# Second-weight combinations by column halves in five regions, and gating remainders one group later

## The chip, the cores and the metric

The kernel runs on one core of one Trainium2 chip. The metric is the device time of one execution in microseconds (us). Engines are named as the profile names them: PE (TensorE), DVE (VectorE), ACT (ScalarE), POOL (GpSimd) and SP (SyncE, whose queue issues every DMA here). Each engine takes its instructions strictly in the order of its own queue.

## The reference

Four batches of 576 positions go through attention, a gated block and a feed-forward block.

```python
x = attention(q, k, v)                     # 8 heads of 64: 4 local (32 back), 4 strided (32 apart)
h = gelu(x @ w_in)                         # 512 -> 1024
u, v = h[..., :512], h[..., 512:]
v = layer_norm(v) * g_ln
x = x + (u * (w_sg @ v + b_sg)) @ w_out    # w_sg: 576 x 576 over positions
y = layer_norm(x) * g_2
out = x + relu(y @ w_ch1) @ w_ch2          # 512 -> 2048 -> 512
```

## The kernel before

**Precision.** Nearly every product is made of three matmuls in a reduced format: an operand is split into a rounded part and a remainder. ACT copies the value into the rounded part, then DVE subtracts it from the value for the remainder (`split`, line 185).

**Attention and gating.** While the gated block of one batch runs, the attention of the next is laid between its groups. For each pair of heads `attn_s` makes scores on PE (`ps_sc`, L373), adds masks on DVE (L383, L384), which carries the scores from PSUM to SBUF, and takes the maxima (`mx`). `attn_e` exponentiates on ACT (L408) and normalises on DVE (`pt`, L418). `attn2` transposes on PE (`ps_t`, L447). The scores have two PSUM banks (`ps_s`), so a pair's scores can start only when the masks of the pair before have been added. `sg_group` makes eight groups per batch: PE fills `ps_g`, DVE multiplies (`z`, L598), ACT copies (`gt`, L599), DVE subtracts (`gt`, L600).

**Feed-forward.** The tokens come in three chunks of 768. In every chunk the first product is made by a seven-product scheme over 2x2 blocks (`product`, L886, seven of six matmuls a pair of column blocks, `pair`, eight pairs). Between a pair's products ACT copies partial sums out of PSUM: `s1` (L938), `u2` (L947) and `u4` (L953). The next product into that bank, `a`, waits for the copy. DVE forms `late` (L954) from the other bank, `b`, to which the pair's last product (number 4) is then added. Chunks 0 and 1 use plain second products (`ch2`); each ends in a late loop of sixteen steps, one `h` (L891, L892) and 12 matmuls a step. Chunk 2 uses seven-product combinations of the second weights too. These are made during chunk 1 by `combine2`, eight times: DVE adds the two parts of `w2` to the whole weight in `stg` (L715), forms combinations in place (L719 to L722), ACT rounds all of it into another part of `stg` (L187), DVE writes the remainder over the sums (L188), and SP stores both in DRAM (`w2_scratch`, L726). One place in `stg` serves all eight.

**Order.** The code is written in program order. A list scheduler then fixes one static order for each engine by its own estimate of when things are ready, so an edit in one place moves instructions in others.

Of the kernel before, what the change touches and what calls it, by code (L numbers as in the profile page):

```python
# [12 lines left out]
F32 = mybir.dt.float32  # L13
F32R = mybir.dt.float32r
U32 = mybir.dt.uint32
AF = mybir.ActivationFunctionType
# [25 lines left out]
NSC = 3  # L42
NLATE = 10
WX = {1: (0, 2, 0), 2: (4, 2, 1), 7: (1, 2, 5), 4: (5, 2, 2), 5: (8, 1, 3), 6: (10, 1, 4), 3: (12, 1, 6)}
WX2 = {1: (0, 2, 0), 2: (4, 2, 2), 7: (1, 2, 1), 4: (5, 2, 2), 5: (8, 1, 0), 6: (10, 1, 1), 3: (12, 1, 3)}
COMBINE_F = {12: 7}
ORDER2 = (1, 7, 2, 6, 5, 4, 3)
XTAGS = (0, 4, 1, 5, 2, 3, 6)
NT = B * S
# [106 lines left out]
def mixer_kernel(ctx: ExitStack, tc: tile.TileContext, io, out):  # L156
# [172 lines left out]
            out=vt[:vrows, :vcols],  # L329
            in_=io["v_l" if local else "v_s"][b, p % (NP // 2)].rearrange("p i h d -> p (i h d)"))  # L330

    pend = {}

    def attn_s(b, p):
        local = p < NP // 2
        n = NLB if local else NSG
        w = LW if local else GW
        if (b, p) not in kv:
            attn_load(b, p)
        qk = kv.pop((b, p))  # L340
        if local:
            p3 = at.tile([P, NLB * LW], F32, tag="pt", name="pt").rearrange("p (n w) -> p n w", w=w)
        else:
            p3 = pts[p % 2].rearrange("p (n w) -> p n w", w=SLOT)[:, :, :w]
        mx = small.tile([P, NSG], F32, tag="mx", name="mx")
        sm = small.tile([P, NSG], F32, tag="sm", name="sm")
        on_pe = b < MASK_PE
        todo = []
        for o in range(2):
            m = (n + 1 - o) // 2  # L350
            if b == 0 and p in START_D:
                ps = ps_d.tile([P, 512], F32, tag="d", name="ps_sc")
            else:
                ps = ps_s.tile([P, 512], F32, tag="s", name="ps_sc")
            lo = 1 if local and o == 0 else 0
            todo.append((slice(o, n, 2), m, ps[:, :m * w].rearrange("p (n w) -> p n w", w=w), lo))
        mk = mask_l[:, 1, :] if local else mask_s
        mkr = mask_lr[:, 1, :] if local else mask_sr
        if on_pe:
            for sl, m, ps3, lo in todo:  # L360
                if lo:
                    nc.tensor.matmul(ps3[:, 0, :], lhsT=ident_r, rhs=mask_lr[:, 0, :], start=True, stop=False,
                                     skip_group_check=True)
                nc.tensor.matmul(ps3[:, lo:, :], lhsT=ident_r,
                                 rhs=mkr.unsqueeze(1).to_broadcast([P, m - lo, w]), start=not lo, stop=False,
                                 skip_group_check=True)
        for i in range(n):
            for h in range(2):
                hs_ = slice(64 * h, 64 * h + 64)
                k0 = KO + QB * i if local else KS + GW * i  # L370
                q0 = QB * i if local else GW * i
                r0 = 64 * (h ^ (i % 2))
                nc.tensor.matmul(todo[i % 2][2][r0:r0 + 64, i // 2, :], lhsT=qk[hs_, q0:q0 + QB],  # L373
                                 rhs=qk[hs_, k0:k0 + w], start=not on_pe, stop=True,
                                 skip_group_check=True)
        chunks = []
        for sl, m, ps3, lo in todo:
            if on_pe:
                masked = ps3
            else:  # L380
                masked = p3[:, sl, :]
                if lo:
                    nc.vector.tensor_tensor(out=p3[:, 0, :], in0=ps3[:, 0, :], in1=mask_l[:, 0, :], op=ALU.add)  # L383
                nc.vector.tensor_tensor(  # L384
                    out=masked[:, lo:, :], in0=ps3[:, lo:, :],
                    in1=mk.unsqueeze(1).to_broadcast([P, m - lo, w]), op=ALU.add)
            nc.vector.tensor_reduce(out=mx[:, sl], in_=masked, op=ALU.max, axis=AX.X)
            if p in SHIFTED[min(b, 1)]:
                nc.vector.tensor_tensor(out=p3[:, sl, :], in0=masked,
                                        in1=mx[:, sl].unsqueeze(2).to_broadcast([P, m, w]), op=ALU.subtract)  # L390
            else:
                nc.vector.tensor_scalar_mul(mx[:, sl], mx[:, sl], -SCALE)
            chunks.append((sl, m, masked))
        pend[b, p] = (p3, n, w, mx, sm, chunks)
# [188 lines left out]
    def sg_group(b, i):  # L583
        u = us[b]
        d, hf = i // 2, i % 2
        if i == 0:
            gts[b] = dw.tile([P, 2, KD, S], F32R, tag="gt", name="gt")
        gt = gts[b]
        dsl = slice(d * P, (d + 1) * P)
        cs = slice(hf * SH, (hf + 1) * SH)  # L590
        ps = ps_d.tile([P, 512], F32, tag="d", name="ps_g")
        o = ps[:, :SH]
        for s in range(4):
            mm3(o, vn[:, 0, s, dsl], vn[:, 1, s, dsl], wsg[:, 0, s, cs], wsg[:, 1, s, cs], s == 0, False)
        nc.tensor.matmul(o, lhsT=vn[:, 1, 4, dsl], rhs=wsg4l[:, cs], start=False, stop=False)
        nc.tensor.matmul(o, lhsT=vn[:, 0, 4, dsl], rhs=wsg4h[:, cs], start=False, stop=True)
        z = dn.tile([P, SH], F32, tag="z", name="z")
        nc.vector.tensor_tensor(out=z, in0=o, in1=u[:, d, cs], op=ALU.mult)  # L598
        nc.scalar.activation(gt[:, 0, d, cs], z, AF.Copy)  # L599
        nc.vector.tensor_tensor(out=gt[:, 1, d, cs], in0=z, in1=gt[:, 0, d, cs], op=ALU.subtract)  # L600

    y_t = {}

    def y_group(b, i):
        gt, x32 = gts[b], x32s[b]
# [101 lines left out]
        (split_later if i + 1 < NW else split)(  # L707
            w[:, 0].rearrange("p k f -> p (k f)"), w[:, 1].rearrange("p k f -> p (k f)"), f)

    def combine2(i):  # L710
        stg = big["stg"]
        c = stg[:, 0:1792].bitcast(F32)
        wf = c[:, 0:1024].rearrange("p (k e r f) -> p k e r f", k=2, e=2, r=2)
        w = w2[i].rearrange("p a k f -> p a (k f)").bitcast(F32)
        nc.vector.tensor_tensor(out=c[:, 0:1024], in0=w[:, 0], in1=w[:, 1], op=ALU.add)  # L715
        s = c[:, 1024:1792].rearrange("p (s e f) -> p s e f", s=3, e=2)
        a11, a21, a12, a22 = wf[:, 0, :, 0], wf[:, 0, :, 1], wf[:, 1, :, 0], wf[:, 1, :, 1]
        tt = nc.vector.tensor_tensor
        tt(out=s[:, 0], in0=a21, in1=a22, op=ALU.add)  # L719
        tt(out=s[:, 1], in0=s[:, 0], in1=a11, op=ALU.subtract)  # L720
        tt(out=a21, in0=a11, in1=a21, op=ALU.subtract)
        tt(out=s[:, 2], in0=a12, in1=s[:, 1], op=ALU.subtract)  # L722
        hi, lo = stg[:, 1792:3584].bitcast(F32R), stg[:, 0:1792].bitcast(F32R)
        split(hi, lo, c)
        for h, src in enumerate((hi, lo)):
            nc.sync.dma_start(out=w2_d[:, :, i, h, :].rearrange("n p f -> p n f"),  # L726
                              in_=src.bitcast(F32).rearrange("p (n f) -> p n f", f=P))

    w2s, slices = {}, {}
# [156 lines left out]
                nc.tensor.matmul(o, lhsT=w[:, a, n0 + nk * k, :], rhs=x[:, c, k, :], start=first and k == 0 and n == 0,  # L886
                                 stop=k == 1 and n == 2, skip_group_check=True)

    def to_h(src):
        h = big["h"].tile([P, 2, TH], F32R, tag="h", name="h")  # L890
        nc.scalar.activation(h[:, 0, :], src, AF.Relu)  # L891
        nc.vector.scalar_tensor_tensor(out=h[:, 1, :], in0=src, scalar=0.0, in1=h[:, 0, :],  # L892
                                       op0=ALU.max, op1=ALU.subtract)
        return h
# [37 lines left out]
    def pair(sc, i, role, mid):  # L932
# [11 lines left out]
        tt(out=c11, in0=c, in1=s1, op=ALU.add)  # L944
        product(sc, i, a, 6, False)
        u2 = tmp("u2")
        nc.scalar.activation(u2, a, AF.Copy)  # L947
        h1 = to_h(c11)
        if i:
            ch2(sc, 0, f1 - 2, 1 - role)  # L950
        product(sc, i, a, 5, False)
# [16 lines left out]
    def steps_at(sc, i, role):  # L968
        if sc + 1 < NSC:
            for step in NORM_AT[sc > 0].get(i, ()):  # L970
                norm(sc + 1, step, role)

    def last_stage():
        for sc in range(NSC - 1):
            role = sc % 2
            for i in range(NW):
                pair(sc, i, role, lambda: steps_at(sc, i - 0.5, role))
                if sc == 0:
                    if i + 2 < NW:
                        prepare(len(units[done[0]:]) if i + 3 == NW else 6)  # L980
                        if i < NW - 2:
                            keep(i + 2)
                else:
                    if i + 2 < NW:
                        fetch(i + 2)
                    if i < NW - len(COMBINE_F):
                        combine2(i)
                steps_at(sc, i, role)
                if i == NW - 3:
                    residual(sc, 0)  # L990
                if i >= NW - 2:
                    rsqrt(sc, i + 2 - NW)
# [6 lines left out]
            for f in range(NF):  # L999
                hs[f] = to_h(late(f))  # L1000
                if f in EXPAND_AT:
                    expand(sc + 1, EXPAND_AT.index(f))
                if f == 4:
                    residual(sc, 1)
                if sc and f in COMBINE_F:
                    combine2(COMBINE_F[f])
                ch2(sc, 1, f, role)
            for d in range(KD):
                leave(sc, 1, d)
# [288 lines left out]
```

## Time and profile before

| quantity | value |
|---|---|
| median of 3 runs | 681.0 us (679.6, 681.0, 681.93) |
| profiled execution, own time | 683.11 us |
| its span | 681.3 us |
| PE busy, share of the span | 655.6 us, 96% |
| DVE busy | 510.1 us, 75% |
| ACT busy | 377.9 us, 55% |

Busy time is the union of an engine's instructions. A gap of PE is time that can be won. [...]

### The profile page before, as it was taken

Reading aid. Unit: us, or ns where it says so; the run is one execution under the profiler, and the core shown is the slowest. Engines: PE = TensorE matmul, PEld = TensorE weight load, DVE = VectorE, ACT = ScalarE, POOL = GpSimd, SP = SyncE. Lnnn points to the kernel's source line nnn. Section 1 sums busy time; section 2 is a strip of 40 time slices with the busy share of each in tenths; the row PEclk is TensorE's granted clock in tenths of the full one; section 3 lists DMA queues with packets and bytes.
Section 4 is the critical chain, followed back from the end, with each engine's and each line's share of the span. In section 5 each row is a group of like instructions: output and inputs, shape, how many; then the busy total and the mean of one; then the engine's idle time right before and its main releaser. Section 6 shows DMA issues by size and latency. Waiting matters only on the chain.

```text
span 681.3 us, 12837 instructions
## 1 busy us (share of the span) xinstructions
PE 655.6 (96%) x4986; PEld 625.9 (92%) x4986; DVE 510.1 (75%) x1026; ACT 377.9 (55%) x884; POOL 18.9 (3%) x24
## 2 busy tenths in 40 slices
PE   5899999999998999999999999999899999999997
PEld 3679989989888988999999999999899999999997
DVE  4989877686758689998989996756679937337983
ACT  3888967283567547645668943333567416447430
POOL 0011011000200011000000000000000000000000
PEclk9999999999997999999999999999999999999999
DMA  8864323457541460449796747899788657665883
GB/s 257 293 175 132 108 96 119 159 155 219 150 144 52 159 209 2 170 160 369 256 349 240 264 177 224 241 285 295 245 250 290 221 160 245 218 221 182 298 283 141
DMA packets 74348, 139.95 MB, mean 205 GB/s; under 512 B 4720, under 2 KB 43888, under 8 KB 73264
## 3 DMA queue, kind: packets, MB, share of 16 engines
q1 hardware_dynamic: 74288, 139.14, 62.1%
q8 instruction: 39, 0.64, 0.4%
q14 instruction: 21, 0.17, 0.1%
HBM read 97.70 MB, written 41.42 MB: 204 GB/s over the span
## 4 chain that ended last, share of the span: by engine, by line
PE 60%; DVE 15%; DMA 14%; ACT 7%; issue 2%; SPq 1%; POOL 1%; DVEq 0%; ACTq 0%; POOLq 0%
PE ps_p L886 16%; PE ps_c L1136 9%; PE ps_o L213 5%; PE ps_o L211 5%; PE ps_o L212 5%; DMA w_scratch<-stg 4%; DMA w_scratch<-w_p 2%; DMA stg<-in_w_ch 2%; PE ps_g L211 2%; PE ps_t L447 2%; PE ps_sc L373 2%; PE ps_g L213 2%; DMA st<-in_w_in 2%; PE ps_g L212 1%; DVE stg L188 1%
## 5 line engine op out<-in xcount | busy, mean ns | idle before, releaser
L886 PE MATMUL ps_p<-x,w 128*128 128x384 f32 x1008 | 185.7, 336 | 4.2 <-ACT u L953 2.3
L886 PEld LDWEIGHTS ps_p<-x,w 128*128 128x128 f32 x1008 | 174.3, 188 | 9.0 <-ACT u L953 3.6
L213 PE MATMUL ps_o<-h,w2p 128*128 128x384 f32 x192 | 64.1, 334 | 0.0
L212 PE MATMUL ps_o<-h,w2p 128*128 128x384 f32 x192 | 64.1, 334 | 0.0
L211 PE MATMUL ps_o<-h,w2p 128*128 128x384 f32 x192 | 63.7, 334 | 0.0
L1136 PE MATMUL ps_c<-t,w2c 128*128 128x384 f32 x288 | 50.3, 335 | 0.0
L1136 PEld LDWEIGHTS ps_c<-t,w2c 128*128 128x128 f32 x288 | 49.9, 188 | 0.3 <-DMA w2c<-w_scratch 0.2
L211 PE MATMUL ps_g<-wsg,vn 128*128 128x288 f32 x128 | 39.8, 311 | 0.0
L213 PE MATMUL ps_g<-wsg,vn 128*128 128x288 f32 x128 | 39.2, 306 | 0.0
L212 PE MATMUL ps_g<-wsg,vn 128*128 128x288 f32 x128 | 38.6, 301 | 0.0
L211 PE MATMUL ps_u<-xhl,winl 128*128 128x288 f32 x128 | 38.1, 297 | 0.0
L211 PE MATMUL ps_y<-gt,wout 128*128 128x288 f32 x128 | 37.7, 297 | 0.0
L213 PE MATMUL ps_u<-xhl,winh 128*128 128x288 f32 x128 | 37.7, 295 | 0.0
L213 PE MATMUL ps_y<-gt,wout 128*128 128x288 f32 x128 | 37.7, 295 | 0.0
L212 PE MATMUL ps_u<-xhl,winh 128*128 128x288 f32 x128 | 37.7, 294 | 0.0
L212 PE MATMUL ps_y<-gt,wout 128*128 128x288 f32 x128 | 37.6, 294 | 0.0
L891 ACT ACTIVATE h<-late 128x384 fp32r<-128x384 f32 x32 | 16.8, 526 | 35.1 <-PE ps_o L213 30.4
L212 PEld LDWEIGHTS ps_o<-h,w2p 128*128 128x128 f32 x192 | 36.0, 188 | 0.0
L213 PEld LDWEIGHTS ps_o<-h,w2p 128*128 128x128 f32 x192 | 36.0, 188 | 0.0
L211 PEld LDWEIGHTS ps_o<-h,w2p 128*128 128x128 f32 x192 | 36.0, 188 | 0.0
L187 ACT ACTIVATE t<-hb 128x768 fp32r<-128x768 f32 x24 | 20.1, 847 | 20.1 <-PE ps_c L1136 19.9
L188 DVE TENSOR_TENSOR t<-hb,t 128x768 fp32r<-128x768 f32 x24 | 22.6, 954 | 5.8 <-ACT t L187 5.8
(235 smaller groups left out, 1588.1 us busy)
## 6 DMA issues: line engine op xcount, KB each, us to landing
w<-w_scratch SPq DMA_DIRECT2D x32, 896.0 KB, 6.9
w_scratch<-w SPq DMA_DIRECT2D x8, 1792.0 KB, 7.8
w_scratch<-stg SPq DMA_DIRECT2D x16, 896.0 KB, 5.9
w2c<-w_scratch SPq DMA_DIRECT2D x28, 512.0 KB, 5.4
stg<-in_w_ch SPq DMA_DIRECT2D x22, 512.0 KB, 6.1
raw_p<-in_w_ch SPq DMA_DIRECT2D x20, 256.0 KB, 3.2
qk<-in_qk_s SPq DMA_DIRECT2D x8, 601.0 KB, 5.0
y_scratch<-y SPq DMA_DIRECT2D x16, 288.0 KB, 2.5
```

The lines of the kernel that those rows point to most:

```text
L187: nc.scalar.activation(dst_h, src, AF.Copy)
L188: nc.vector.tensor_tensor(out=dst_l, in0=src, in1=dst_h, op=ALU.subtract)
L211: nc.tensor.matmul(ps, lhsT=ll, rhs=rh, start=first, stop=False)
L212: nc.tensor.matmul(ps, lhsT=lh, rhs=rl, start=False, stop=False)
L213: last_mm[0] = nc.tensor.matmul(ps, lhsT=lh, rhs=rh, start=False, stop=last)
L373: nc.tensor.matmul(todo[i % 2][2][r0:r0 + 64, i // 2, :], lhsT=qk[hs_, q0:q0 + QB], rhs=qk[hs_, k0:k0 + w], start=not on_pe, stop=True, sk ...
L447: nc.tensor.transpose(ps[:rows, (t - t0) * c:(t - t0 + 1) * c], src, ident)
L886: nc.tensor.matmul(o, lhsT=w[:, a, n0 + nk * k, :], rhs=x[:, c, k, :], start=first and k == 0 and n == 0, stop=k == 1 and n == 2, skip_gro ...
L891: nc.scalar.activation(h[:, 0, :], src, AF.Relu)
L1136: nc.tensor.matmul(ps[m, e][:, :TH], lhsT=w[:, i, a, :], rhs=x[:, c, :], skip_group_check=True, start=m not in (2, 3) and i == 0 and k == ...
```

## The change

Gating: a group's remainder (`low`) is now issued during the next group, after its `z`, and is ordered behind the last mask addition that has been written so far. Second weights: `combine2(i, e)` makes one column half; 16 halves take their two areas in turn from five regions of 896 columns. DRAM rows are renumbered so that a half is seven adjacent ones (`WX2`, and the store). Halves are written at the middle of a pair (`half_way`) and at its end, and the last two at steps 10 and 13 of the late loop of chunk 1. In `pair` the rounded `h1` is ordered behind the `u2` copy.

```diff
-COMBINE_F = {12: 7}
+COMBINE_F = {10: (7, 0), 13: (7, 1)}
...
         nc.vector.tensor_tensor(out=z, in0=o, in1=u[:, d, cs], op=ALU.mult)
+        if i:
+            lows.pop()()
         nc.scalar.activation(gt[:, 0, d, cs], z, AF.Copy)
-        nc.vector.tensor_tensor(out=gt[:, 1, d, cs], in0=z, in1=gt[:, 0, d, cs], op=ALU.subtract)
+
+        def low():
+            op = nc.vector.tensor_tensor(out=gt[:, 1, d, cs], in0=z, in1=gt[:, 0, d, cs], op=ALU.subtract)
+            if last_mask[0] is not None:
+                tc.add_manual_dep(op.ins, last_mask[0].ins.name, ORDER, reason="scores leave PSUM first")
+
+        lows.append(low)
+        if i == 7:
+            lows.pop()()
...
-    def combine2(i):
+    def combine2(i, e):
         stg = big["stg"]
-        c = stg[:, 0:1792].bitcast(F32)
...
+        n = 2 * (2 * i + e)
+        c, hi = (stg[:, 896 * (j % 5):896 * (j % 5) + 896] for j in (n, n + 1))
+        lo, c, hi = c.bitcast(F32R), c.bitcast(F32), hi.bitcast(F32R)
...
+        tt(out=wf, in0=w[:, 0, :, e], in1=w[:, 1, :, e], op=ALU.add)
...
         split(hi, lo, c)
         for h, src in enumerate((hi, lo)):
-            nc.sync.dma_start(out=w2_d[:, :, i, h, :].rearrange("n p f -> p n f"),
+            nc.sync.dma_start(out=w2_d[7 * e:7 * e + 7, :, i, h, :].rearrange("n p f -> p n f"),
                               in_=src.bitcast(F32).rearrange("p (n f) -> p n f", f=P))
...
-        h1 = to_h(c11)
+        h1 = to_h(c11, snap)
...
+    def half_way(sc, i, role):
+        steps_at(sc, i - 0.5, role)
+        if sc and i:
+            combine2(i - 1, 1)
```

On DVE, at gating groups 0 and 1 of the third batch (second pair of heads of the fourth batch), the order before is:

```order
L598 TENSOR_TENSOR z<-ps_g,u 128x288
L600 TENSOR_TENSOR gt<-z,gt 128x288
L598 TENSOR_TENSOR z<-ps_g,u 128x288
L600 TENSOR_TENSOR gt<-z,gt 128x288
L384 TENSOR_TENSOR pt<-ps_sc,mask_l 128x4x96
L383 TENSOR_TENSOR pt<-ps_sc,mask_l 128x96
L384 TENSOR_TENSOR pt<-ps_sc,mask_l 128x4x96
```

In the changed kernel the same place on DVE reads as follows, up to the normalisation of the first pair (L418):

```order
L598 TENSOR_TENSOR z<-ps_g,u 128x288
L604 TENSOR_TENSOR gt<-z,gt 128x288
L598 TENSOR_TENSOR z<-ps_g,u 128x288
L384 TENSOR_TENSOR pt<-ps_sc,mask_l 128x4x96
...
L411 TENSOR_SCALAR sm<-sm 128x9
L392 TENSOR_SCALAR mx<-mx 128x5
L598 TENSOR_TENSOR z<-ps_g,u 128x288
L412 RECIPROCAL sm<-sm 128x9
L604 TENSOR_TENSOR gt<-z,gt 128x288
L418 TENSOR_TENSOR pt<-pt,sm 128x864
```

The second remainder has moved from ahead of three mask additions to nearly last.

On SP, at the end of chunk 0's late loop, the order before, from the load of chunk 2's normed rows (`yc`) on, is:

```order
L817 DMA yc<-y_scratch 128x4x768
L726 DMA w_scratch<-stg 128x14x128 x3
L927 DMA out<-yr 128x384 x2
L726 DMA w_scratch<-stg 128x14x128
L919 DMA yr<-y_scratch 128x384 x2
```

In the changed kernel SP has there:

```order
L829 DMA yc<-y_scratch 128x4x768
L738 DMA w_scratch<-stg 128x7x128 x11
L941 DMA out<-yr 128x384 x2
L738 DMA w_scratch<-stg 128x7x128
L933 DMA yr<-y_scratch 128x384 x2
```

Three stores of 896 KB have become eleven of 448 KB ahead of the same output stores.

On DVE, in the first pair of chunk 1, the order before from its first sum (`c`) is:

```order
L944 TENSOR_TENSOR c_5351<-ps_p_5344,s_5335 128x384
L892 SCALAR_TENSOR_TENSOR h<-c_5351,h 128x384
L954 TENSOR_TENSOR late<-ps_p_5337,u_5370 128x384
```

In the changed kernel it is (L729 is the addition that opens a half, here of halves 7 and 8, counted from 0):

```order
L958 TENSOR_TENSOR c_5351<-ps_p_5344,s_5335 128x384
L732 TENSOR_TENSOR stg<-stg 128x128
L729 TENSOR_TENSOR stg<-w2p_4374 128x512
L733 TENSOR_TENSOR stg<-stg 128x128
L906 SCALAR_TENSOR_TENSOR h<-c_5351,h 128x384
L734 TENSOR_TENSOR stg<-stg 128x128
L735 TENSOR_TENSOR stg<-stg 128x128
L732 TENSOR_TENSOR stg<-stg 128x128
L729 TENSOR_TENSOR stg<-w2p_4374 128x512
L968 TENSOR_TENSOR late<-ps_p_5337,u_5370 128x384
```

Eight rows of combinations now stand between `c` and `late`; before there were none.

## Rows read from the trace of the kernel before

**Rows 1.** The page, busy us by engine.

```profile
PE 655.6 (96%) x4986; PEld 625.9 (92%) x4986; DVE 510.1 (75%) x1026; ACT 377.9 (55%) x884; POOL 18.9 (3%) x24
```

**Rows 2.** Waits of PE, 60 to 660 us: total, times, longest.

```profile
PE ps_sc L373 <- DVE pt L384: 3.1, 4, 2.1
PE ps_p L886 <- ACT u L953: 2.3, 3, 1.7
```

**Rows 3.** Timeline of PE from 203.3 us: start, duration, idle before.

```profile
205.75 0.32 PE L373 MATMUL ps_sc<-qk 64*64 64x54 f32 x4 [2.12 <-DVE pt L384]
206.47 0.43 PE L373 MATMUL ps_sc<-qk 64*64 64x54 f32 x5 [0.40 <-DVE pt L384]
```

**Rows 4.** Timeline of DVE, 203 to 206.6 us.

```profile
203.01 0.45 DVE L598 TENSOR_TENSOR z<-ps_g,u 128x288 f32<-128x288 f32 x1
204.76 0.46 DVE L600 TENSOR_TENSOR gt<-z,gt 128x288 fp32r<-128x288 f32 x1 [1.30 <-ACT gt L599]
205.14 0.55 DVE L384 TENSOR_TENSOR pt<-ps_sc,mask_l 128x384 f32<-128x384 f32 x1
...
205.77 0.55 DVE L384 TENSOR_TENSOR pt<-ps_sc,mask_l 128x384 f32<-128x384 f32 x1
```

**Rows 5.** Windows: length, busy of PE, PEld, DVE, ACT, POOL; clock, DMA share, GB/s.

```profile
204.00:206.00 2.00, 0.25 (x4) 0.20 (x4) 1.24 (x4) 1.81 (x10) 0.00 (x0) 1.00 0.69 233
206.00:208.00 2.00, 1.60 (x45) 1.46 (x42) 2.00 (x8) 0.55 (x3) 0.00 (x0) 0.50 0.06 24
...
212.00:214.00 2.00, 2.00 (x40) 1.64 (x39) 0.87 (x5) 0.51 (x2) 0.00 (x0) 0.80 0.00 0
```

**Rows 6.** Timeline of ACT from 207 us: the second pair's exponentials begin.

```profile
207.45 0.37 ACT L408 ACTIVATE pt<-pt,mx 128x96 f32<-128x96 f32 x1 [1.64 <-DVE mx L392]
```

**Rows 7.** Timeline of DVE, 207 to 209.1 us: the first pair's normalisation.

```profile
207.32 0.17 DVE L411 TENSOR_SCALAR sm<-sm 128x9 f32<-128x9 f32 x1
...
208.07 1.06 DVE L418 TENSOR_TENSOR pt<-pt,sm 128x864 f32<-128x864 f32 x1
```

**Rows 8.** Timeline of DVE, 486 to 494 us: one combination of chunk 1.

```profile
487.73 1.23 DVE L715 TENSOR_TENSOR stg<-w2p 128x1024 f32<-128x1024 f32 x1 [2.10 <-DMA w_scratch<-stg]
488.88 0.55 DVE L944 TENSOR_TENSOR c<-ps_p,s 128x384 f32<-128x384 f32 x1
...
490.95 0.42 DVE L721 TENSOR_TENSOR stg<-stg 128x256 f32<-128x256 f32 x1
491.29 0.42 DVE L722 TENSOR_TENSOR stg<-stg 128x256 f32<-128x256 f32 x1
```

**Rows 9.** Timeline of ACT at the same place.

```profile
491.74 1.70 ACT L187 ACTIVATE stg<-stg 128x1792 fp32r<-128x1792 f32 x1 [0.95 <-DVE stg L722]
493.34 0.47 ACT L953 ACTIVATE u<-ps_p 128x384 f32<-128x384 f32 x1
```

**Rows 10.** Timeline of PE at the same place.

```profile
493.87 1.31 PE L886 MATMUL ps_p<-x,w 128*128 128x384 f32 x6 [1.72 <-ACT u L953]
```

**Rows 11.** Window of the pairs of chunk 1, columns as in group 5.

```profile
440.00:520.00 80.00, 77.21 (x438) 75.32 (x437) 55.38 (x92) 40.81 (x71) 0.00 (x0) 1.00 0.89 277
```

**Rows 12.** Windows in chunk 0's late loop, columns as in group 5.

```profile
419.00:422.00 3.00, 3.00 (x19) 3.00 (x18) 0.92 (x2) 0.53 (x1) 0.00 (x0) 1.00 1.06 297
425.00:428.00 3.00, 3.00 (x19) 3.00 (x18) 1.95 (x5) 1.70 (x1) 0.00 (x0) 1.00 0.00 0
```

**Rows 13.** DMA issues, 409 to 424 us: KB, us to landing.

```profile
yc<-y_scratch SPq DMA_DIRECT2D x1, 1536.0 KB, 6.9
```

**Rows 14.** DMA issues, 448 to 460 us, beside loads of first weights.

```profile
w_scratch<-stg SPq DMA_DIRECT2D x1, 896.0 KB, 10.3
```

**Rows 15.** Timeline of SP: the load of `yc` is issued.

```profile
409.97 0.37 SPq L817 DMA_DIRECT2D yc<-y_scratch  x1
```

**Rows 16.** Timeline of DVE in the first pair of chunk 1.

```profile
434.54 0.56 DVE L954 TENSOR_TENSOR late<-ps_p,u 128x384 f32<-128x384 f32 x1 [0.94 <-ACT u L953]
436.97 0.56 DVE L962 TENSOR_TENSOR c<-ps_p,u 128x384 f32<-128x384 f32 x1 [1.88 <-PE ps_p L886]
```

More of the change, by code (lines that the diff above doesn't have):

```diff
@@ L44 @@
 WX = {1: (0, 2, 0), 2: (4, 2, 1), 7: (1, 2, 5), 4: (5, 2, 2), 5: (8, 1, 3), 6: (10, 1, 4), 3: (12, 1, 6)}
-WX2 = {1: (0, 2, 0), 2: (4, 2, 2), 7: (1, 2, 1), 4: (5, 2, 2), 5: (8, 1, 0), 6: (10, 1, 1), 3: (12, 1, 3)}
-COMBINE_F = {12: 7}
+WX2 = {1: (0, 7, 0), 2: (2, 7, 2), 7: (1, 7, 1), 4: (3, 7, 2), 5: (4, 7, 0), 6: (5, 7, 1), 3: (6, 7, 3)}
+COMBINE_F = {10: (7, 0), 13: (7, 1)}
 ORDER2 = (1, 7, 2, 6, 5, 4, 3)
@@ L330, in attn_load_v @@
             in_=io["v_l" if local else "v_s"][b, p % (NP // 2)].rearrange("p i h d -> p (i h d)"))
-    pend = {}
+    pend, last_mask = {}, [None]
     def attn_s(b, p):
@@ L383, in attn_s @@
                     nc.vector.tensor_tensor(out=p3[:, 0, :], in0=ps3[:, 0, :], in1=mask_l[:, 0, :], op=ALU.add)
-                nc.vector.tensor_tensor(
+                last_mask[0] = nc.vector.tensor_tensor(
                     out=masked[:, lo:, :], in0=ps3[:, lo:, :],
@@ L598, in sg_group @@
         nc.vector.tensor_tensor(out=z, in0=o, in1=u[:, d, cs], op=ALU.mult)
+        if i:
+            lows.pop()()
         nc.scalar.activation(gt[:, 0, d, cs], z, AF.Copy)
-        nc.vector.tensor_tensor(out=gt[:, 1, d, cs], in0=z, in1=gt[:, 0, d, cs], op=ALU.subtract)
+        def low():
[5 more added lines that the diff above has]
+            lows.pop()()
     y_t = {}
+    lows = []
     def y_group(b, i):
@@ L708, in second @@
             w[:, 0].rearrange("p k f -> p (k f)"), w[:, 1].rearrange("p k f -> p (k f)"), f)
-    def combine2(i):
+    def combine2(i, e):
         stg = big["stg"]
-        c = stg[:, 0:1792].bitcast(F32)
[L713 to L717, printed above, removed]
-        tt = nc.vector.tensor_tensor
-        tt(out=s[:, 0], in0=a21, in1=a22, op=ALU.add)
-        tt(out=s[:, 1], in0=s[:, 0], in1=a11, op=ALU.subtract)
+        n = 2 * (2 * i + e)
+        c, hi = (stg[:, 896 * (j % 5):896 * (j % 5) + 896] for j in (n, n + 1))
+        lo, c, hi = c.bitcast(F32R), c.bitcast(F32), hi.bitcast(F32R)
+        tt = nc.vector.tensor_tensor
+        wf = c[:, 0:512].rearrange("p (k f) -> p k f", k=2)
+        w = w2[i].rearrange("p a k (e f) -> p a k e f", e=2).bitcast(F32)
+        tt(out=wf, in0=w[:, 0, :, e], in1=w[:, 1, :, e], op=ALU.add)
+        a11, a21, a12, a22 = (c[:, k * P:(k + 1) * P] for k in range(4))
+        s = [c[:, k * P:(k + 1) * P] for k in range(4, 7)]
+        tt(out=s[0], in0=a21, in1=a22, op=ALU.add)
+        tt(out=s[1], in0=s[0], in1=a11, op=ALU.subtract)
         tt(out=a21, in0=a11, in1=a21, op=ALU.subtract)
-        tt(out=s[:, 2], in0=a12, in1=s[:, 1], op=ALU.subtract)
-        hi, lo = stg[:, 1792:3584].bitcast(F32R), stg[:, 0:1792].bitcast(F32R)
+        tt(out=s[2], in0=a12, in1=s[1], op=ALU.subtract)
         split(hi, lo, c)
         for h, src in enumerate((hi, lo)):
-            nc.sync.dma_start(out=w2_d[:, :, i, h, :].rearrange("n p f -> p n f"),
+            nc.sync.dma_start(out=w2_d[7 * e:7 * e + 7, :, i, h, :].rearrange("n p f -> p n f"),
                               in_=src.bitcast(F32).rearrange("p (n f) -> p n f", f=P))
@@ L887, in product, with to_h @@
                                  stop=k == 1 and n == 2, skip_group_check=True)
-    def to_h(src):
+    def to_h(src, behind=None):
         h = big["h"].tile([P, 2, TH], F32R, tag="h", name="h")
-        nc.scalar.activation(h[:, 0, :], src, AF.Relu)
+        op = nc.scalar.activation(h[:, 0, :], src, AF.Relu)
+        if behind is not None:
+            tc.add_manual_dep(op.ins, behind.ins.name, ORDER, reason="snapshot first")
         nc.vector.scalar_tensor_tensor(out=h[:, 1, :], in0=src, scalar=0.0, in1=h[:, 0, :],
@@ L946, in pair @@
         u2 = tmp("u2")
-        nc.scalar.activation(u2, a, AF.Copy)
-        h1 = to_h(c11)
+        snap = nc.scalar.activation(u2, a, AF.Copy)
+        h1 = to_h(c11, snap)
         if i:
@@ L976, in last_stage @@
             for i in range(NW):
-                pair(sc, i, role, lambda: steps_at(sc, i - 0.5, role))
+                pair(sc, i, role, lambda: half_way(sc, i, role))
                 if sc == 0:
@@ L985, in last_stage @@
                         fetch(i + 2)
-                    if i < NW - len(COMBINE_F):
-                        combine2(i)
+                    if i < NW - 1:
+                        combine2(i, 0)
                 steps_at(sc, i, role)
@@ L1005, in last_stage @@
                 if sc and f in COMBINE_F:
-                    combine2(COMBINE_F[f])
+                    combine2(*COMBINE_F[f])
                 ch2(sc, 1, f, role)
```

## The prediction

> **What bounds the kernel now.** I read the page first: PE is busy in 655.6 of 681.3 us [rows 1], so only what shortens PE's 25.7 us of gaps, or its time at the lower clock, can show. Next the list of PE's waits away from both ends: the two largest entries are scores waiting for a mask addition, 3.1 us, and first products waiting for the `u4` copy, 2.3 us [rows 2]. These are the two places that the change touches, and the timelines show how each wait comes about.
>
> At 203.63 us PE stops, for 2.12 us and then 0.40, because the second pair's masks have not emptied the banks [rows 3]. DVE has its `z` at 203.46, but the next row in its queue is the remainder L600, which waits 1.30 us for its rounded copy on ACT; only then come the masks, at 205.14 and 205.77 [rows 4]. [...] The window from 212 reads 0.80, so the rise came near 212.8 [rows 5]: 6.8 us at half clock.
>
> At 487.73 a whole combination opens after DVE has idled 2.10 us for the store that held `stg` [rows 8]. Its rounding on ACT waits another 0.95 us and takes 1.70, `u4` stands right behind it at 493.34 [rows 9], and PE has lost 1.72 us [rows 10]. PE's gaps in the pairs of chunk 1 come to 80.00 - 77.21 = 2.8 us [rows 11].
>
> **Gating remainders.** The order shows the second remainder gone from ahead of the masks. The first mask can start at 203.46 instead of 205.14, 1.7 us earlier, and the scores with it: the 2.12 us becomes about 0.45. The 0.40 stays, for it is the time to the next mask.
>
> If the clock then stays at 1.00, up to half of the 6.4 us in which PE worked from 206 to 212.8 (6.8 less the 0.4 idle in the first of those windows) could go as well, 3.2 us. I don't count all of it, since something else is late next. The transposes that come soon after the next groups' first matmuls need the first pair's normalised `pt`, which ended at 208.07 + 1.06 = 209.13 [rows 7]. L411 ahead of it could not have run before the last exponential of that pair, at 207.45 - 1.64 = 205.81 [rows 6]; it ran at 207.32 because of DVE's queue. With the masks 1.7 us earlier it comes near 205.9, and with one remainder of 0.46 us now ahead, `pt` ends about 208.1, 1.0 us earlier than before. So PE gets a new wait of about a microsecond there. The second pair's exponentials come 1.6 us earlier, the ACT idle of [rows 6]. I take 2.6 us: 1.7, and 0.9 of the 3.2. The ends are 0, if ACT and DVE rather than PE set the stretch, and 4.9.
>
> The other DVE rows of the gating are moved and not added. In the last batch the remainders of groups 6 and 7 come one DVE operation later, when DVE has no spare time; I put 0.3 us on PE (0 to 0.9, twice the 0.46 us of a remainder [rows 4]), since the second output group needs both.
>
> **Halves in five regions.** A half's addition now waits for a store two to three halves back, not for the one just made, so the 2.10 us should go. The rounding of 896 columns takes about half of 1.70 us. In ACT's new order a rounding stands directly ahead of `u4` only in the second pair. I take 2.0 of the 2.8 us, with ends 0.5, if only the halving of 1.70 counts, and 2.8.
>
> What it adds: six more DVE instructions a combination, 48 in all. The start-to-start times are 1.15 us for 1024 columns (487.73 to 488.88) and 0.34 for 256 (490.95 to 491.29) [rows 8]; a straight line through them leaves 0.07 us that doesn't shrink with the columns, so 3.4 us in all. DVE's idle 80.00 - 55.38 = 24.6 us [rows 11] hides it; without that cover it would delay `c`, `h` and `late`, and PE with them. The added eight roundings of ACT hide likewise (40.81 busy of 80). The 16 added stores cost SP some 0.37 us each to issue, as the `yc` load does [rows 15], 5.9 us over more than 90, none of it on a full queue. The order of `u2` ahead of `h1` costs nothing where it already held, and `h1` then waits for one copy of 0.5 us, which twelve matmuls cover.
>
> **The price of being early.** The order puts eleven half stores on SP between `yc` and chunk 0's output stores, and eight DVE rows ahead of the first `late` of chunk 1. The DMA engines have room: no traffic at 425 to 428 [rows 12]. A half store is 459 kB, at 297 GB/s [rows 12] 1.54 us. `yc` is issued at 409.97 [rows 15] and took 6.9 us with a store beside it [rows 13]; I start the stores at 416. The eleventh lands at 416 + 11 x 1.54 = 433. Half 8 opens in the region that it empties, and behind that addition (0.7 us) stands `late`, which ran at 434.54 [rows 16]. So the store leaves 0.8 us to spare. The eight rows themselves take about 2.7 us on DVE after `c`, which puts `late` near 435.5. The last product waits for it and ended just before 436.97 [rows 16]; six matmuls of 0.17 us ahead of that is 435.9. I take 0.4 us lost. The ends are 0 and 2.4: if the output stores' 1.2 MB (six of 192 KB) went first, the eleventh would land 4 us later, and of that 435.9 - 0.7 - 0.6 - 433 = 1.6 us is covered (0.7 for the addition, 0.6 for `late`).
>
> [...]
>
> **Sum.** -2.6 - 2.0 + 0.3 + 0.4 = -3.9 us. The profiled execution took 683.11 us, so it would take 679.2. The median of the runs is 2.1 us below it: 677.1 us.
>
> **Rivals.**
>
> (a) The clock falls again. PE's waits at this place would still be about 0.45, 0.4 and 1.0 us, and the trace shows it falling after 2.12 and 0.40. The masks' 1.7 us stays, the 0.9 doesn't: -3.0, 678.0; with only half of the second gain, 679.0. [...]
>
> (b) The gating gain is hidden anyway. From 204 to 206 ACT is busy 1.81 of 2.00 us [rows 5], so it may be ACT that sets when the attention ends, and PE waits later instead. Or the fall belongs to the profiled execution, which is 2.1 us above the median. Then only 2.0 - 0.7 is left: 679.7. Against it: ACT idles 1.64 us right behind [rows 6].
>
> (c) Slower: stores drain too slowly for the early halves. DVE stands in order at the addition of half 8, with `late` behind it and PE behind that. It costs nothing up to a pace of (435.9 - 0.7 - 0.6 - 416) / 11 = 1.7 us a half store and 11 us for each further 1. At 2.3 us it costs 6.7 in place of the 0.4 above: -2.6 - 2.0 + 0.3 + 6.7 = +2.4, 683.4. For it: one store of 896 KB took 10.3 us to land beside loads of weights [rows 14], 5.2 a half. Against it: those loads are issued only after the first pair is done.
>
> **How the numbers follow.** Forecast 0.52, (a) 0.20, (b) 0.17, (c) 0.11. A measurement of this kernel can tell about 0.3% from no change, 2.0 us, so faster is below 679.0 and slower above 683.0. The forecast and two thirds of (a) are faster, 0.65; the rest of (a) and (b) the same, 0.24; (c) slower, 0.11. The range goes from 681.0 - 4.9 - 2.8, rounded up to 673.5, to 681.0: it holds all but (c) and the outer ends. The forecast's own range is 674.5 to 679.
>
> **What would show it.** After: the mask row follows `z` directly near 203.5 us, PE's wait for L384 falls from 3.1 to about 1.4 us, and the clock reads 1.00 there; waits for the `u4` copy fall below 0.8 us; DVE has next to no idle time ahead of the opening additions. A clock of 0.50 in the same place, PE waiting for `late` by more than 1 us, or DVE standing at an opening addition in chunk 0's late loop would make the prediction wrong.

## The result, and the profile after

The changed kernel takes 675.73 us, median of 6 runs (674.61 to 678.56), against 681.12 us for the kernel before: a ratio of 0.9909, 95% interval 0.9882 to 0.9936, or 5.4 us less. Timed once more beside the experiments, it took 675.19 us against 681.56 (0.9911, interval 0.9884 to 0.9937). 677.1 us had been predicted, with a range of 673.5 to 681.0. Single executions of one kernel lie up to 8 us apart, so profiled executions are compared below by stretches and not by their spans. The profiled execution of the changed kernel took 676.41 us, its span 674.6.

The first lines answer to [rows 1] and [rows 2]: the page's busy times, and the whole list of PE's waits from 60 to 660 us.

```profile
PE 653.2 (97%) x4986; PEld 624.4 (93%) x4986; DVE 512.1 (76%) x1074; ACT 379.4 (56%) x892; POOL 18.9 (3%) x24
...
PE ps_m L837 <- DVE sr L814: 1.7, 2, 0.9
PE ps_sc L373 <- DVE pt L384: 1.4, 4, 0.4
PE ps_t L447 <- DVE pt L418: 1.1, 1, 1.1
PE ps_t L447 <- ACT x L495: 0.8, 2, 0.4
PE ps_pv L466 <- ACT pT L455: 0.7, 1, 0.7
PE ps_p L898 <- ACT s L1049: 0.2, 1, 0.2
```

The wait for the masks has gone from 3.1 to 1.4 us, the wait for the `u4` copy is no longer listed, and a new one of 1.1 us for `pt` has come. The same place in the timelines of PE (first fence) and DVE (second), which answer to [rows 3, 4, 7]:

```profile
204.34 0.32 PE L373 MATMUL ps_sc<-qk 64*64 64x54 f32 x4 [0.40 <-DVE pt L384]
205.02 0.80 PE L373 MATMUL ps_sc<-qk 64*64 64x54 f32 x40 [0.35 <-DVE pt L384]
...
208.31 0.94 PE L447 MATMUL ps_t<-ident,pt 128*96 128x128 f32 x7 [1.09 <-DVE pt L418]
```

```profile
203.33 0.45 DVE L598 TENSOR_TENSOR z<-ps_g,u 128x288 f32<-128x288 f32 x1
203.70 0.55 DVE L384 TENSOR_TENSOR pt<-ps_sc,mask_l 128x384 f32<-128x384 f32 x1
...
204.33 0.55 DVE L384 TENSOR_TENSOR pt<-ps_sc,mask_l 128x384 f32<-128x384 f32 x1
...
206.80 0.40 DVE L604 TENSOR_TENSOR gt<-z,gt 128x288 fp32r<-128x288 f32 x1
207.12 1.05 DVE L418 TENSOR_TENSOR pt<-pt,sm 128x864 f32<-128x864 f32 x1
```

The mask follows its `z` at once. The remainder has moved to 206.80 and stands ahead of `pt`, which the transposes wait for. Windows of the changed kernel, which answer to [rows 5, 11] (length, busy PE, PEld, DVE, ACT, POOL; the granted clock of TensorE as a share of full speed, DMA share, GB/s):

```profile
206.00:208.00 2.00, 1.22 (x9) 0.99 (x8) 1.84 (x6) 2.00 (x12) 0.00 (x0) 1.00 0.02 10
208.00:210.00 2.00, 1.69 (x17) 1.55 (x17) 2.00 (x7) 2.00 (x11) 0.00 (x0) 1.00 0.03 8
...
400.00:440.00 40.00, 40.00 (x229) 39.29 (x228) 36.81 (x82) 17.08 (x29) 0.00 (x0) 1.00 0.91 264
440.00:520.00 80.00, 79.91 (x460) 79.34 (x459) 58.71 (x117) 44.39 (x80) 0.00 (x0) 1.00 0.91 290
```

The clock stays at 1.00, and in the pairs of chunk 1 PE idles 0.1 us where it idled 2.8. In the other three profiles with halves, five regions and the order of `h1` it idles 0.0, 0.5 and 1.5 us in the same window. One more view: everything from the first `ps_m` of the last stage that waits for `sr` to the end of the span, first of the kernel before and then of the changed one.

```profile
263.46:681.30 417.84, 408.87 (x2390) 402.97 (x2390) 311.35 (x519) 211.44 (x363) 0.92 (x1) 1.00 0.70 236
```

```profile
261.38:674.60 413.22, 407.88 (x2390) 403.12 (x2390) 314.88 (x567) 212.83 (x371) 0.92 (x1) 1.00 0.70 239
```

The same 2390 matmuls take 4.6 us less: PE idles 5.3 us instead of 9.0, and is shown busy 1.0 us less.

### The profile page after: what moved, and what is told of

Read it like the earlier page. It is cut to its first block, busy times and chain, and to the rows that moved or that the text cites. A ratio compares the mean times of both kernels' runs of the same rounds, so it can differ in the third digit from the quotient of the medians.

```text
span 674.6 us, 12948 instructions
## 1 busy us (share of the span) xinstructions
PE 653.2 (97%) x4986; PEld 624.4 (93%) x4986; DVE 512.1 (76%) x1074; ACT 379.4 (56%) x892; POOL 18.9 (3%) x24
## 4 chain that ended last, share of the span: by engine, by line
PE 70%; DMA 11%; DVE 8%; ACT 7%; issue 2%; SPq 1%; POOL 1%; ACTq 0%; DVEq 0%; POOLq 0%
PE ps_p L898 21%; PE ps_c L1155 7%; PE ps_o L213 5%; PE ps_o L211 5%; PE ps_o L212 5%; DMA w_scratch<-w_p 3%; DMA stg<-in_w_ch 2%; PE ps_y L213 2%; PE ps_y L211 2%; PE ps_y L212 2%; PE ps_g L211 2%; PE ps_g L213 2%; PE ps_g L212 2%; PE ps_t L447 2%; PE ps_pv L466 1%
## 5 line engine op out<-in xcount | busy, mean ns | idle before, releaser
L211 PE MATMUL ps_g<-wsg,vn 128*128 128x288 f32 x128 | 39.1, 305 | 0.0
L213 PE MATMUL ps_g<-wsg,vn 128*128 128x288 f32 x128 | 38.5, 301 | 0.0
L212 PE MATMUL ps_g<-wsg,vn 128*128 128x288 f32 x128 | 38.2, 298 | 0.0
L211 PE MATMUL ps_v<-winh,xhl 128*128 128x512 f32 x64 | 25.3, 396 | 2.1 <-DVE xhl L503 1.9
```

The costliest lines, as they stand in the source:

```text
L211: nc.tensor.matmul(ps, lhsT=ll, rhs=rh, start=first, stop=False)
L212: nc.tensor.matmul(ps, lhsT=lh, rhs=rl, start=False, stop=False)
L213: last_mm[0] = nc.tensor.matmul(ps, lhsT=lh, rhs=rh, start=False, stop=last)
```

## The experiments

Two stretches make single profiles comparable. **Gating** is the time from the start of the second pair's scores (the row x40 above, 206.47 us in [rows 3]) to the start of the transposes that wait for L495, here of the kernel before and then of the changed one:

```profile
228.45 0.66 PE L447 MATMUL ps_t<-ident,pts 128*128 128x128 f32 x4 [0.39 <-ACT x L495]
```

```profile
225.71 0.66 PE L447 MATMUL ps_t<-ident,pts 128*128 128x128 f32 x4 [0.38 <-ACT x L495]
```

It begins behind the wait for the masks and does not hold it. **Last stage** is the stretch shown above. Times are in us; the ratio is to the kernel before; a dash stands where a profile joins the row x40 to the one ahead of it, or where there was one execution.

```
kernel                        median   ratio, 95% interval     gating   last stage
before                        681-682  1                       21.98    417.84
before, second profile        -        -                       20.43    418.63
order of h1 alone             681.79   1.0000 0.9978-1.0022    20.73    417.37
gating part alone             679.28   0.9952 0.9930-0.9975    20.68    416.75
halves alone                  677.14   0.9930 0.9907-0.9952    20.16    413.69
changed, without mask order   676.43   0.9918 0.9886-0.9951    21.03    413.74
changed                       675.73   0.9909 0.9882-0.9936    20.69    413.22
changed, again                675.19   0.9911 0.9884-0.9937    20.69    413.55
four regions                  676.61   0.9920 0.9892-0.9947    20.69    414.02
without the order of h1       677.66   0.9945 0.9924-0.9967    -        415.86
halves in their own pair      678.89   0.9960 0.9937-0.9983    -, 20.69 415.49, 416.01
three regions                 682.94   1.0029 1.0009-1.0048    -        420.39
two regions                   684.40   1.0051 1.0028-1.0074    20.68    422.30
```

**The two parts by themselves.** The first kernel adds only the gating lines of the diff to the kernel before. The second is the changed kernel with

```diff
-        if i:
-            lows.pop()()
         nc.scalar.activation(gt[:, 0, d, cs], z, AF.Copy)
-        def low():
...
+        nc.vector.tensor_tensor(out=gt[:, 1, d, cs], in0=z, in1=gt[:, 0, d, cs], op=ALU.subtract)
```

> The kernel before with the gating part of the change alone (remainders one group later and behind the mask additions); the combinations stay whole. My theory, from the two traces: the gating part is worth 1.7 us of wait and 1.3 us of clock less the new wait, so 3.0 us below the kernel before, about 678.1 us against 681.1; in its profile PE waits about 0.4 us and 0.35 us for the second pair's masks near 204 us, about 1.1 us for the normalised pt, the granted clock there reads 1.00, and the chunk-1 pairs still lose about 2.8 us of PE. Rival 1 (the fall of the clock belongs to single executions, not to the wait): only the 1.7 us show in the median, 679.4. Rival 2 (most of the gain is the early halves, the gating is hidden): within 1 us of before, 680.1 or more.

> The changed kernel with the old gating: halves in five regions alone. My theory: the pairs of chunk 1 give back their 2.8 us of PE gaps and the late sums of chunk 0 some 0.5 us more, with nothing paid for the early halves, so 2.7 to 3.3 us below before, about 678.0; in its profile PE still waits about 2.1 us for the second pair's masks near 204 us, the granted clock falls to 0.50 behind it, and 440 to 520 us has PE busy for 79.5 us or more. Rival 1 (fall of the clock by chance): the wait is there and the clock stays 1.00. Rival 2 (halves and gating only work together, the halves need the time that the gating frees): 1.5 us or less, 679.6 or more. The two effects add up to the whole change (5.4 us in the medians) by my theory; by rival 2 their sum falls short by 2 us or more.

Gating alone gives 2.0 us in the medians (the ratio says 3.3, interval 1.7 to 4.8), halves alone 4.1 (ratio 4.8, interval 3.3 to 6.3). Of the gating's two theories the rival with 679.4 is nearer than mine with 678.1. The parts add up to the whole within their intervals, so nothing shows that one needs the other. The halves are worth more than my theory had. Whole combinations with more than one place in `stg`, and the renumbered rows or the new places of the last two halves by themselves, were not run. In the profile of the gating alone chunk 1 still has waits of the old size. The longest is for `u2` (L958) this time, as it is in the second profile of the kernel before with 2.6 us; the second row is for `u4`:

```profile
461.76 1.32 PE L897 MATMUL ps_p<-x,w 128*128 128x384 f32 x6 [1.70 <-ACT u L958]
489.69 1.32 PE L897 MATMUL ps_p<-x,w 128*128 128x384 f32 x6 [1.06 <-ACT u L964]
```

In that of the halves alone the mask wait is there, and the clock did not fall, as rival 1 had it:

```profile
209.09 0.32 PE L373 MATMUL ps_sc<-qk 64*64 64x54 f32 x4 [2.12 <-DVE pt L384]
...
208.00:210.00 2.00, 0.52 (x17) 0.42 (x20) 1.89 (x5) 1.15 (x7) 0.00 (x0) 1.00 0.26 103
210.00:212.00 2.00, 1.87 (x48) 1.58 (x42) 1.97 (x8) 1.21 (x6) 0.00 (x0) 1.00 0.00 0
```

**The order behind the masks, and the clock.** One kernel is the changed one without the order:

```diff
-            if last_mask[0] is not None:
-                tc.add_manual_dep(op.ins, last_mask[0].ins.name, ORDER, reason="scores leave PSUM first")
```

The other is the kernel before, profiled once more.

> The changed kernel with the remainders issued one group later, but without the order behind the mask additions; the static order then puts the second remainder ahead of the second pair's masks again, as before the change. My theory: the order behind the masks carries the whole gating gain, so PE waits about 2 us near 204 us, the clock falls to 0.50 there and 2.5 to 3 us are lost against the changed kernel: 678.2 to 678.7. Rival 1 (the wait without the clock's part, since the clock falls by chance): 1.7 us lost, 677.4. Rival 2 (later remainders are enough, their rounded copies being done by then): no more than 0.5 us lost, 676.2.

> The kernel before, one more profiled execution, to see whether the clock falls again behind the wait for the second pair's masks near 204 us. Theory 1 (the wait of 2 us sets it off in most executions): a wait of 2.1 us and a granted clock of 0.50 behind it. Theory 2 (it fell there by chance): the wait, and 1.00 behind it; the stretch from the masks to the first products of the last values is then 1.5 to 2 us shorter than the 21.0 us of the first profile.

Without the order DVE's list again has the remainder ahead of the masks, and the wait is back in full, at 204.45 us. Issuing the remainder later does nothing there by itself; the order alone, without issuing it later, was not run. The clock falls behind it, but for a shorter time than in [rows 5], and so it does in the second profile of before. PE of the kernel without the order, its windows, and then the windows of before, second profile:

```profile
204.45 0.32 PE L373 MATMUL ps_sc<-qk 64*64 64x54 f32 x4 [2.08 <-DVE pt L384]
...
206.00:208.00 2.00, 1.63 (x9) 1.31 (x10) 1.97 (x8) 1.84 (x10) 0.00 (x0) 0.65 0.00 0
208.00:210.00 2.00, 2.00 (x10) 1.91 (x11) 1.99 (x8) 2.00 (x12) 0.00 (x0) 0.50 0.03 8
210.00:212.00 2.00, 2.00 (x45) 1.60 (x46) 1.15 (x4) 1.19 (x4) 0.00 (x0) 0.99 0.00 0
```

```profile
208.00:210.00 2.00, 0.85 (x24) 0.75 (x28) 2.00 (x6) 0.81 (x6) 0.00 (x0) 0.77 0.21 84
210.00:212.00 2.00, 2.00 (x37) 1.90 (x30) 1.97 (x7) 1.54 (x8) 0.00 (x0) 0.50 0.00 0
212.00:214.00 2.00, 2.00 (x17) 2.00 (x16) 2.00 (x7) 2.00 (x12) 0.00 (x0) 0.88 0.00 0
```

Of the five profiled executions with this 2.1 us wait the clock fell here in four; of the nine without it, in none. The wait sets it off, mostly. What the fall costs is in the table's gating column: 21.98 in the first profile of before, 20.43, 20.73 and 21.03 with a shorter fall, 20.16 with none, and 20.68 or 20.69 in every one with the new gating, which has the new wait of 1.1 us for `pt`. In four of the five the kept clock and the new wait nearly cancel. The median of the kernel without the order is 0.7 and 1.2 us above the two of the changed one, with overlapping intervals: they could not be told apart by time, and my theory of 678.2 to 678.7 missed. That the wait is back is shown by the profile alone.

**How many regions.** The changed kernel with two, three and four regions in place of five, here two:

```diff
-        c, hi = (stg[:, 896 * (j % 5):896 * (j % 5) + 896] for j in (n, n + 1))
+        c, hi = (stg[:, 896 * (j % 2):896 * (j % 2) + 896] for j in (n, n + 1))
```

> The changed kernel with two regions in place of five, so that every half opens in the region that the half just before it still stores. My theory: the regions do most of it. DVE stands at the opening additions for the stores again, a half store of some 5 us from issue to landing, the roundings come late and stand ahead of the u4 copies, so 1 to 2 us of the 2.7 us in chunk 1's pairs are lost, and the early halves in chunk 0's late loop hold up late sums: 677 to 679 us. Rival (halving alone does it, because a rounding of 0.9 us instead of 1.7 fits between the copies): within 0.5 us of the changed kernel, 675.7 to 676.2.

> The changed kernel with three regions in place of five. With two, the additions that open a half wait 22.8 us for stores between 400 and 560 us and the kernel takes 684.4. Theory 1 (what counts is how far the halves can run ahead of the stores, which take 5 to 6.5 us each to land whatever their size): with three, a half's rounding opens in the region whose store was made one half before, fewer than the eleven halves of the changed kernel fit ahead of chunk 1's pairs, and DVE still waits for stores for some 8 to 12 us: 677.5 to 680. Theory 2 (it is enough that the opening addition does not wait for the store made just before): as the changed kernel, 675.5 to 676.5.

> The changed kernel with four regions in place of five: each half then has one of two sets of its own, and its opening addition and its rounding wait for the stores of two halves before. So far two regions gave 684.4 us, three 682.9, five 675.2 and 675.7. Theory 1 (the time follows how many halves fit ahead of the stores): between three and five, 677.5 to 680, with ACT and DVE waiting for stores between 400 and 560 us by more than the 10 to 13 us of ACT and 3 to 5 us of DVE that five show. Theory 2 (what three regions lose is only that a rounding writes where the half just before still stores, which four no longer do): as five, 675 to 676.5.

Halves with two regions are slower than whole combinations. I had expected them between the two kernels, and for three regions neither theory had more than 680. With two, DVE waits longest for stores, and PE then for DVE (3.0 us for `o`, `h` and `late` between 400 and 600 us). With three it is ACT, whose rounding writes where the half just before is still being stored. Waits from 400 to 560 us of the kernel before and of two, three and five regions in turn:

```profile
DVE stg L715 <- DMA w_scratch<-stg: 9.2, 5, 3.9
```

```profile
DVE stg L729 <- DMA w_scratch<-stg: 22.8, 13, 3.1
```

```profile
ACT stg L187 <- DMA w_scratch<-stg: 27.6, 11, 4.8
```

```profile
ACT stg L187 <- DMA w_scratch<-stg: 10.5, 7, 2.3
...
DVE stg L729 <- DMA w_scratch<-stg: 2.9, 2, 1.6
```

With three regions a `u` copy stands behind a rounding that waits, and PE behind the copy. From its timeline:

```profile
499.98 1.33 PE L898 MATMUL ps_p<-x,w 128*128 128x384 f32 x6 [1.71 <-ACT u L961]
...
515.95 1.33 PE L898 MATMUL ps_p<-x,w 128*128 128x384 f32 x6 [1.64 <-ACT u L967]
```

Halving did not halve the time that a store takes here. DMA issues from 400 to 580 us of two regions and of five (KB each, median us to landing); whole ones took 5.9 in the same stretch of the kernel before:

```profile
w_scratch<-stg SPq DMA_DIRECT2D x32, 448.0 KB, 5.0
```

```profile
w_scratch<-stg SPq DMA_DIRECT2D x32, 448.0 KB, 6.5
```

So with two regions DVE waits 13 times in place of 5, each time about as long (1.75 us for 1.84). What keeps a half store from landing in half the time was not shown; other transfers were under way (DMA share 0.89 from 440 to 520 us in the kernel before [rows 11], 0.91 with five regions).

The time of four regions cannot be told from that of five; it is 0.1 us above the range of theory 2. DVE waits 12.0 us for stores there, and PE is behind those waits in part: it loses 1.5 us at two `u2` copies that stand behind a rounding. For one of them the chain is in the trace. DVE's opening addition (first fence) waits for a store, the rounding on ACT then waits 3.84 us for DVE's combinations, and PE (second fence) waits for the copy behind it:

```profile
447.00 0.69 DVE L729 TENSOR_TENSOR stg<-w2p 128x512 f32<-128x512 f32 x1 [2.64 <-DMA w_scratch<-stg]
```

```profile
450.56 1.31 PE L898 MATMUL ps_p<-x,w 128*128 128x384 f32 x6 [0.55 <-ACT u L961]
```

Between three and four lie 6.3 us. With four, a half never writes where the half just before is being stored.

**Running ahead.** Each half is held in its own pair of chunk 1:

```diff
-        tt(out=wf, in0=w[:, 0, :, e], in1=w[:, 1, :, e], op=ALU.add)
+        op = tt(out=wf, in0=w[:, 0, :, e], in1=w[:, 1, :, e], op=ALU.add)
+        tc.add_manual_dep(op.ins, last_late[0].ins.name, ORDER, reason="in its own pair")
...
-        tt(out=late(f2), in0=b, in1=u4, op=ALU.add)
+        last_late[0] = tt(out=late(f2), in0=b, in1=u4, op=ALU.add)
```

> The changed kernel with five regions, but each half's opening addition ordered behind the late sum of the pair in whose code it stands, so that no half runs ahead into chunk 0's late loop: two halves lie in each pair of chunk 1. Theory 1 (the run-ahead empties the pairs, and that is where the 2.8 us of gaps go): the roundings stand between the copies again and the pairs lose 1 to 2.5 us of PE: 676.7 to 678.2, with waits for u2, u4 or s1 copies of 0.5 us or more in the profile. Theory 2 (with five regions no store is waited for and a rounding of 0.9 us fits between the copies): no wait for the copies over 0.5 us, 675.2 to 676.2.

> The kernel with every half in its own pair, one more profiled execution: its first profile was among its shortest executions (676.7 us where the median is 678.9), with 2 us of gaps behind 400 us. Theory 1 (the longer executions lose their time in chunk 1's pairs, where the DMA engines were busy all the time in the first profile): more gaps between 440 and 520 us, 3 us or more, at waits for copies that stand behind a rounding. Theory 2 (they lose it in the first 60 us, as other kernels do): gaps behind 400 us of about 2 us again.

3.2 to 3.7 us are lost in the medians and 1.9 to 2.8 in the last stage. Running ahead brings about half of what the halves bring. Theory 1 had the direction, and 676.7 to 678.2 us for the 678.9 measured. PE's waits are for the `s1` copy (0.9 and 1.2 us in the two profiles) and for DVE's `h` (0.9 and 1.3). One row of the first kind from each profile:

```profile
446.18 1.15 PE L901 MATMUL ps_p<-x,w 128*128 128x384 f32 x5 [0.93 <-ACT s L955]
```

```profile
498.79 1.32 PE L901 MATMUL ps_p<-x,w 128*128 128x384 f32 x6 [0.87 <-ACT s L955]
```

The two last stages differ by 0.5 us and the two spans by 6.0 (674.9 and 680.9), so what parts them lies ahead of the last stage: 4.9 us of it are there by the first L595 matmul behind 60 us (63.59 and 68.46). That was theory 2 of the second profile.

**The order of `h1`.** The changed kernel without it, and the kernel before with it alone:

```diff
-        h1 = to_h(c11, snap)
+        h1 = to_h(c11)
```

> The changed kernel without the order of h1's rounding behind the u2 copy. Theory 1 (the order costs and brings nothing, as the prediction had it): within 0.7 us of the changed kernel, 675.0 to 676.4. Theory 2 (without it h1 stands ahead of u2 in some pairs and the copy is late): a wait for u2 of 0.4 to 0.6 us in two or three pairs, 676.5 to 677.5.

> The kernel before with one line of the change alone: the rounding of h1 ordered behind the u2 copy. Theory 1 (the line is worth something by itself, because in some pairs of the kernel before ACT's order has h1 ahead of u2, and the wait of 0.47 us for u2 at 465 us goes): 0.5 to 1.5 us below before, about 680.3. Theory 2 (it matters only with the early halves, where roundings would otherwise crowd the first pair of chunk 1): within 0.5 us of before, 681.0 to 681.8.

Alone it is worth nothing that can be measured. With the halves it is worth 1.9 to 2.5 us in the medians, 2.3 to 2.6 in the last stage, a little more than theory 2 had. Without it a half's rounding and that of `h1` stand ahead of `u2` in the first pair of chunk 1, and the same two ahead of `s1` in a later one:

```profile
428.67 1.50 PE L898 MATMUL ps_p<-x,w 128*128 128x384 f32 x7 [1.23 <-ACT u L961]
...
470.29 1.34 PE L898 MATMUL ps_p<-x,w 128*128 128x384 f32 x6 [1.07 <-ACT s L952]
```

**The changed kernel again.**

> The changed kernel itself, timed again beside the three below, since single executions of one kernel lie up to 7 us apart. By what its own runs gave: 675.7 us median, 5.4 us below the kernel before. Nothing is told apart by it but the size of the whole.

It confirmed the size, and its profile has one wait that the first has not. DVE and PE in the first pair of chunk 1:

```profile
432.76 0.68 DVE L729 TENSOR_TENSOR stg<-w2p 128x512 f32<-128x512 f32 x1
433.36 0.55 DVE L968 TENSOR_TENSOR late<-ps_p,u 128x384 f32<-128x384 f32 x1
```

```profile
433.96 1.34 PE L898 MATMUL ps_p<-x,w 128*128 128x384 f32 x6 [0.83 <-DVE late L968]
```

## Why the prediction was right, and where its sizes were off

**Gating, -2.6: the mechanism was right, the clock's part too large.** The 2.12 and 0.40 us became 0.40 and 0.35, so 1.8 for the 1.7 predicted, and in five of the nine profiles with the new gating the two came to 0 to 0.33, which the prediction had not seen, since it kept the 0.40. The new wait of a microsecond behind one remainder came as worked out, 1.09. The 0.9 us for the kept clock rested on one execution with a long fall. There it came to 1.3 (21.98 less 20.69); in the other four with the wait it came to between -0.5 and +0.3. Rival (b) was right in this half: most of that gain belonged to the profiled execution. A longer stretch takes in the waits of both pairs, from the last L595 ahead of the first pair's scores (199.28 us before, 199.56 in the changed kernel) to the same transposes: 26.9 to 29.2 us in the five profiles with the wait, 24.3 to 26.2 in the nine without, with means of 27.7 and 25.0. So the size of 2.6 was nearly right, but most of it lies in the waits; that they made up for the clock's 0.9 is luck. Rival (a), a clock that falls again, did not occur at this place in any of the nine profiles with the new gating. With the wait of 2.1 us the fall did follow, four times in five, but one fall cost 1.8 us at most against the execution without one (21.98 less 20.16).

**Last batch, +0.3: it cost nothing.** The last batch's groups run from 271 to 290 us, inside the last stage. Group 7's remainder ends there later than before, as worked out (288.41 us in the changed kernel and 289.64 before, 27.0 and 26.2 us behind the start of the stage), but no output group waits for it: PE's list of waits has no entry for `gt`. PE starts the last matmul of the output groups at these places, in the kernel before and in the changed one:

```profile
300.27 0.29 PE L213 MATMUL ps_y<-gt,wout 128*128 128x288 f32 x1
```

```profile
298.02 0.29 PE L213 MATMUL ps_y<-gt,wout 128*128 128x288 f32 x1
```

Behind the start of the last stage that is 36.8 us in the four profiles with the old gating and 36.6 to 36.7 in the ten with later remainders. A stretch that is 0.3 us longer in the means does exist, from the transposes behind L495 to the first `ps_m` that waits for `sr` (35.0 to 35.5 us before, 35.4 to 35.7 after), but no group of the last batch lies in it. 0.13 of it is one L595 matmul that PE now does behind the transposes and not ahead of them, the rest a longer wait for `sr`.

**Halves, -2.0: mis-sized; this is the step that made the gain larger than forecast.** The last stage is 4.1 us shorter (a mean of 417.6 in the four profiles with whole combinations, 413.6 in the four with halves, five regions and the order of `h1`). The prediction counted only the gaps in the pairs of chunk 1 and took 2.0 of them; 2.7 went in the first changed profile, and 2.3 in the means of the same profiles (2.8 to 0.5 us from 440 to 520 us). So that term was nearly right, and what the prediction left out is the rest: about 2.8 of the 4.1 is idle time of PE in the whole stage (8.7 to 6.0 us in the same means), and 1.3 is shown as busy: a product behind a wait is a row of 1.32 us, as above in the gating part alone, and without one, in the changed kernel, of 1.20:

```profile
450.99 1.20 PE L898 MATMUL ps_p<-x,w 128*128 128x384 f32 x6
```

That the restart of PE behind each wait accounts for all of the 1.3 is argued from such rows only. Stores are still waited for: DVE's opening additions wait 2.9 us, where the prediction had next to nothing, and ACT's roundings 10.5, which it had not counted. In the first changed profile no wait of PE stands behind them.

Two sentences of that part failed. "The order of `u2` ahead of `h1` costs nothing" was right as a cost, and missed that without it the early halves lose some 2.4 us again. And the lower end of 0.5 took the halving for a gain if the regions brought nothing: halving with two regions is a loss of 3.1 us against the kernel before, so that end had no ground.

**The price of being early, +0.4: it is there in some executions.** 0.83 us in the second changed profile, none in the first, and none in those of the halves alone and of the kernel without the mask order. The eleven half stores were issued from 408.0 us on and not from 416, behind a `yc` load that came 4 us earlier, and PE was busy 40.00 of 40.00 us around them. SP of the first changed profile, which answers to [rows 15]:

```profile
405.81 0.37 SPq L829 DMA_DIRECT2D yc<-y_scratch  x1
408.00 18.87 SPq L738 DMA_DIRECT2D w_scratch<-stg  x11
```

**Rival (c), stores too slow,** is a real mechanism of this kernel. It decides below four regions, and with three it sits on ACT. The prediction had looked for it in front of DVE's opening additions alone.

**Sum.** By stretches: -2.1 for the second pair's masks (2.5 us of waits, and 0 to 0.8 with the new gating, 0.4 in the mean), -0.1 behind them, +0.3 to the last stage, -4.1 in it, in all -6.0 us; the two medians say -5.4 and -6.4. The -3.9 predicted was short by 1.5 to 2.5, and the shortfall lies in the halves with their price, -4.1 for -1.6. That is why the time came out below the 677.1 us forecast, though inside the range.

## What to carry to other kernels

Before you cut a piece of staged work smaller, count the places that it is staged in. A store of 448 KB took about as long to land here (medians of 5.0 and 6.5 us) as one of 896 KB (5.9), and the halves paid only where no piece writes where the one just before is still on its way out (676.6 us with four regions, 682.9 with three). Where a static order may run work ahead, one order edge on a short copy that the bottleneck waits for can be worth half of what the restructuring brings (some 2.4 of 4.1 us here), though it is worth nothing alone. Compare profiles by stretches between the same two instructions, since spans of one kernel differed by 6 us for reasons ahead of the stretch that was changed.

## What the runs showed of the hardware that was not expected

The clock also falls near the start in some executions, and there it can cost little. In the second profile of the changed kernel PE reads 0.63 from 10 to 20 us (and about 0.85 from 20 to 30 and from 40 to 50), and yet it comes to its first L595 matmul behind 60 us only 1.3 us later than in the first profile (65.02 for 63.72), whose clock stays at 1.00:

```profile
10.00:20.00 10.00, 7.30 (x121) 5.85 (x123) 9.10 (x28) 7.38 (x28) 0.00 (x0) 0.63 0.98 352
```

The kernel before and the halves alone both read 1.00 up to 200 us and lie 3.1 us apart at the same matmul (63.19 and 66.26). The second profile with every half in its own pair reads 0.66 from 40 to 50 us and comes to it 4.9 us behind the first (68.46 for 63.59); PE is busy for only 8.0 us of that window, and how much the clock has of the delay is not shown. The mean clock of an execution therefore does not tell its time by itself. The same wait of 2.1 us was followed by a fall of about 7 us, by shorter ones, and once by none.
